# Another order, and another choice of engine, for the VectorE, ScalarE and GpSimd work of an attention, Fourier and MLP kernel

## The chip, the cores and the metric

The kernel runs on one core of one Trainium2 chip. A core has five engines with an instruction queue each: TensorE (PE in the profile, with its weight loads as PEld), VectorE (DVE), ScalarE (ACT), GpSimd (POOL) and SyncE (SP), which here issues nearly all DMA transfers. Each engine works through its own list strictly in order, and waits at semaphores for what other engines and transfers make. The metric is the device time of the whole program in microseconds (us).

## The reference

First comes attention with random features, for 8 batches and 8 heads of 576 positions by 64; then a Fourier mix of its output over positions and channels, a normalisation, and an MLP of 512 to 2048 to 512:

```
def phi(x):
    proj = np.einsum('bhsd,md->bhsm', x, omega)
    sq = np.sum(x * x, axis=-1, keepdims=True) / 2.0
    h = proj - sq
    h = h - np.max(h, axis=-1, keepdims=True)
    return np.exp(h) / np.sqrt(m)
...
num = np.einsum('bhsm,bhmd->bhsd', q_p, kv)
den = np.einsum('bhsm,bhm->bhs', q_p, z)[..., None] + 1e-06
...
X = np.fft.fft(x, axis=1)
X = np.fft.fft(X, axis=2)
u = x + np.real(X)
...
ch = np.maximum(un @ w_ch1, 0.0) @ w_ch2
return (u + ch).astype(np.float32)
```

The two weight matrices come as 64-bit floats, and the kernel turns them into 32-bit ones itself.

## The kernel before

The program has two parts. The first (to about 433 us in the profile) does the attention for 32 pairs of heads, the Fourier mix of 8 batches, the conversion of the weights, the MLP of the first four tiles of 128 rows (called plain), and the preparation of the weights for the second part. The second part does the MLP of the other rows with a recursive product scheme that saves multiplications (lines from 1640 on). The change touches the first part alone.

Nothing in the first part is a plain loop. Each piece of work is a generator that yields steps; a step names the engines that it may run on with a planned cost for each, the events that it waits for, the buffers and PSUM banks that it takes and gives back, and the event that it makes. The planner (class `Listing`, method `run`) holds one step of every open stream in a list, and writes steps down one by one; when it writes a step, the code behind the `yield` issues the step's instructions. In the first part it does not choose: the string PICKS says which stream comes next and which of the step's engines takes it, one character for each step. A character's index in DIGITS is divided by 36: the remainder is the place of the stream in the list, the quotient the engine in the step's own order. So PICKS fixes the order of every engine's queue. Planned costs then matter no more; the chip's waits come from semaphores that follow from what each step reads and writes. BANKS fixes, in the order of the takes, which PSUM bank is used.

The steps that the change and the prediction speak of:

- Transposes of a pair's k and q rows and of its features on TensorE (L608), copied out of PSUM in blocks by `evicted` (L622 and L624), on ScalarE or VectorE; `kqT` and `qeT` are the results.
- Feature products (L702), then in `softmax` the row maximum on VectorE (L645) and the exponentials on ScalarE (L662, four for a group).
- k-features times v (L736), kept by `keep` (L750 VectorE, L752 ScalarE); numerators and denominators (L783, L791); the division (L800 to L812).
- `narrow`: the conversion of one slab of 512 weight columns, of 32. Its first step scales the high words (L533 GpSimd, or L535 ScalarE), three steps on VectorE treat the bits (L538, L540 and L543, L545), and the last adds (L551, GpSimd or VectorE). It reads the tile `raw`, one of four slab buffers, and the last step gives the buffer back. The load of a later slab (L565, SyncE) waits for a buffer.
- `folds`: sums and differences over mirrored positions and channels ahead of the Fourier products (L839, L845, L855, L868), VectorE or GpSimd; the products (L897 to L945); copies of the spectra on ScalarE (L918).
- `residual` and `summed`: the spectrum is mirrored and added to x (L989 on ScalarE, L994 and L997 on VectorE, L1006 and L1007 on VectorE or GpSimd), then written to DRAM (L976, L1021, L1032, SyncE).
- Normalisation of a tile (L1163 to L1169), its transposed rows `unT` (L1177), the first MLP layer (L1237), its copies in `hidden` (L1221 VectorE, L1223 ScalarE), the second layer (L1260).
- `op` in `w2_parts`: differences of the second weight matrix for the second part (L1485, VectorE or GpSimd).

SyncE's list interleaves the loads of k and q (L472, L475, two buffers), of v (L480, three buffers), of the slabs, and the traffic of the mix. A load that must wait for a buffer holds back all that stands behind it. Some preparation for the second part is started after given numbers of listed steps (the string BETWEEN); all of those numbers lie past the region that the change touches.

Of the kernel before, what the change touches and what calls it, by code (L numbers as in the profile page):

```python
# [41 lines left out]
class Clock(NamedTuple):  # L42
# [23 lines left out]


PICKS = (
    "40e0fff03eafdaege3OcdceefdcOdeccfgda37ghj0gjj7hlP79aj7ik97i8S7efhjffeHldffiehdjfdOihgihidaKedbhhciff"
    "ecgOfeejdfdPdeeedgifdffdefd8aiii88jhd8jP8b99i8e8jcddghjgheiifcOcdciieicgPgdefJcdghbkededfgcRbggb79ij"  # L70
    "8hi7hjafN9Haj9gfffeg8eif8hcej1jccc7ehidbhffLigebfbe6766gggfcbjahj9Ofghhjj8dQkkgT6jghff8de6dUjfhbgegh"
    "cefhafjUf8jgciSjOckkhjakkaeikggjlioklnhSgodoXON7l7l6nnj9icadc97cibf98ejH88a7edhMlhkmjjaQVijihkkfplSm"
    "okliljjilVaghVhnmljkmpjkhhnmkimlgglmbjpjjQ9d9alafhhdjlaMdjback0j766k7lh4g896ck6gkki77gij5ijhgj6dimni"
    "3ndjgi6Kc4jldlKikbkaijLhf75dcjlmklk36ci45jciekajkkkk5kihokeaeoLaioNlencidonbSiljjcmjjkboijTUUhgcfkik"
    "hiflkmeFF99nol5m8jT7naabda89Rbj97ecdl8cjilOgifkQb4acahg57ebbgabgdjkdTkk6eceebb5f9dg4R6ce486ggg6egfhh"
    "fg4g9egf5cbdhgPRhhcgjhggejigibLmHnbedijj6NOb7biihi9bgihMkaffPa8cijdhbdghbaeibNefffacjicigifi99975ih5"
    "jgj8699ajfg6g7fgefd65bO6Kalkkgd5jgjikagfldliPJpeoaeeefgdejadgilgScljiii5e65k56kl57k7j67S9lilk9gliih6"
    "ffkgec4fg4dbgg7fedaiP5gfbheefilddddddeghg9kbfncgghcfkkafkagGngb65p5Hopoj4bhoanbelli68bjjl5b7dlhighhi"
    "lflhpkgiWomjknmmmkimnjbjhn9jkmFKkfFgedccff6Wf7idUVhi8Th3fogbqp8fgmkeSdjna7ckenoghmnmffnjeo79q6547oa4"
    "nlkpd7aceonnc8blSVicilbhmjim8fh7SnnIl5mUkfjgfhhfhihg8ghfbS4kjf83j4lllb79jei8mnkblfnmmiolpilOUi9Mh5l5"  # L80
    "pmnaem79jjVmkbblek5iji9a9kffTgjikhiShfgjafhgfigh4g50PPP0ba5Pdh9dghdK77hgfdcbg8OO988jMehefibjjkellfcc"
    "PcdhQMihfQcffbKCf82b3c98cbcdcd6a299efgddbJaGQQbefLa9ecf74gg986HRgf9idg8kQeheff7be6ff2e5cc8fbcgdKP8f8"
    "9hN9Lc999bddcHcNb7Oc9effegd7ibhQeQ8haf7ccghhlUikhHW5lWmm5dkMQGM71fS6d1gdb99747ifddhIfdhhdhfdbihgiljn"
    "gWgijgg93ekKl8kEhIIbT3jjKgkb9k9eTfhkhlje34m49974iG66h68faHe6e7a79982975aI94a39c8cM8b4aa7ab984fge8eLM"
    "98b86ce8PbFPc9cbe6cKPf3a9b94fIdIQeJKbd876eJPdc5fNb7ffbf9JSS8RiLa4a7gPbajfgg8gdfhg2i2787Hf6OcdIN5d3LH"
    "accd46ddeKK72dJc7bbaa4bb9a9bc7c0777dghhdf7Bfddebd76ff1fddIe9949438686bc6aca85348dHcG7a5be957b55d1544"
    "9Gc1F5a9a68446344584584E59189970955888574443113301110"
)
# [2307 lines left out]
```

## Time and profile before

| what | value |
|---|---|
| median of 3 runs | 1124.67 us (1122.62 to 1125.05) |
| the profiled execution | 1126.43 us |
| its span, first to last instruction | 1124.6 us |
| granted TensorE clock | 1.000 |
| first part, 0 to 433 us: TensorE busy | 422.68 us |
| the same: VectorE, ScalarE, GpSimd busy | 353.31, 306.46, 192.19 us |

The profile is one execution. Its page gives the busy time of each engine, groups of instructions by line and tile, and the chain of work that ended last; the trace behind it answers for stretches of time, for single lines and for waits. A row of the timeline reads: start in us, length in us, engine, line, operation, what it writes and reads, shapes, how many; in brackets the idle time before it and what ended that. Matmul ends are modelled, so a busy TensorE still holds short stalls.

### The profile page before, as it was taken

To read this page: it belongs to the slowest core of one execution; us is meant where nothing else is said; L and a number is where in the kernel's file an instruction comes from. 1 tells how busy PE (TensorE), PEld (TensorE's weight loads), DVE (VectorE), ACT (ScalarE), POOL (GpSimd) and SP (SyncE) were. 2 spreads that over 40 slices of the span, in tenths; PEclk is the share of its full clock that TensorE was granted. 3 is DMA by queue.
4 is the path that set the end of the run, shared out by engine and by line. 5 is a ranking of instruction groups with operands and counts; after the bars stand their busy time and mean duration, and the time that the engine had idled before them with its cause. 6 is when DMAs were issued, how large, how long until landed. Compare 5 with 4: busy or idle time off the path is not lost.

```text
span 1124.6 us, 31666 instructions
## 1 busy us (share of the span) xinstructions
PE 1109.1 (99%) x12467; PEld 1000.3 (89%) x12467; DVE 887.5 (79%) x1684; ACT 540.6 (48%) x1644; POOL 389.5 (35%) x402
## 2 busy tenths in 40 slices
PE   8999999999999999999999999999999999999998
PEld 7888888879869678899999889999889999889998
DVE  6999999987676766687697777888667898668895
ACT  7998898856635465624214553223563222341221
POOL 2443443644473347633513454000365000142000
PEclk9999999999999999999999999999999999999999
DMA  8866766565675659798898768757778757546553
GB/s 234 217 194 181 229 188 211 156 206 166 215 231 183 191 164 317 239 301 277 240 297 287 215 203 255 201 155 234 208 209 250 219 156 218 165 155 216 150 160 105
DMA packets 196549, 236.13 MB, mean 210 GB/s; under 512 B 53808, under 2 KB 120624, under 8 KB 196400
## 3 DMA queue, kind: packets, MB, share of 16 engines
q1 hardware_dynamic: 195904, 233.83, 68.7%
q8 instruction: 99, 1.62, 0.6%
q14 instruction: 50, 0.41, 0.1%
q10 hardware_dynamic: 496, 0.26, 0.1%
HBM read 182.13 MB, written 56.10 MB: 212 GB/s over the span
## 4 chain that ended last, share of the span: by engine, by line
PE 88%; DVE 3%; DMA 3%; ACT 3%; POOL 1%; issue 1%; SPq 1%; DVEq 0%; POOLq 0%; ACTq 0%
PE banks L2179 30%; PE banks L1728 26%; PE banks L1237 5%; PE banks L702 5%; PE banks L608 4%; PE banks L1879 3%; PE banks L1260 3%; PE banks L736 2%; PE banks L783 2%; PE banks L945 2%; DMA raw<-in_moe_w_ch_dram 1%; PE banks L895 1%; ACT e L662 1%; DVE nmx L645 1%; PE banks L905 1%
## 5 line engine op out<-in xcount | busy, mean ns | idle before, releaser
L2179 PE MATMUL banks<-wl,sums 128*128 128x128 f32 x1792 | 219.8, 275 | 0.5 <-issue 0.5
L2179 PEld LDWEIGHTS banks<-wl,sums 128*128 128x128 f32 x1792 | 210.6, 192 | 1.5 <-issue 0.9
L662 ACT ACTIVATE e<-banks,nmx 128x128 f32<-128x128 f32 x576 | 165.2, 429 | 25.0 <-DVE nmx L645 24.3
L645 DVE TENSOR_REDUCE nmx<-banks 128x8 f32<-128x1024 f32 (+1 forms) x96 | 89.2, 950 | 17.6 <-PE banks L702 13.4
L2179 PE MATMUL banks<-wl,hid 128*128 128x128 f32 x768 | 99.2, 275 | 0.3 <-DVE part L2155 0.3
L2179 PEld LDWEIGHTS banks<-wl,hid 128*128 128x128 f32 x768 | 92.9, 192 | 0.9 <-DVE part L2155 0.5
L2150 ACT ACTIVATE s<-banks 128x128 f32<-128x128 f32 x112 | 30.9, 277 | 113.6 <-PE banks L2179 103.5
L1728 PE MATMUL banks<-unw,wxw 128*128 128x256 f32 x352 | 85.5, 379 | 0.0
L702 PE MATMUL banks<-om,kqT 64*64 64x128 f32 (+1 forms) x2088 | 78.7, 275 | 2.2 <-ACT kv L752 1.4
L702 PEld LDWEIGHTS banks<-om,kqT 64*64 64x64 f32 (+1 forms) x2088 | 64.1, 138 | 13.2 <-issue 3.4
L2179 PE MATMUL banks<-wl,hx 128*128 128x128 f32 x576 | 74.2, 275 | 0.4 <-DVE part L2155 0.4
L1728 PEld LDWEIGHTS banks<-unw,wxw 128*128 128x128 f32 x352 | 66.6, 190 | 8.9
L1728 PE MATMUL banks<-rx,wxw 128*128 128x256 f32 x288 | 70.8, 379 | 0.0
L1753 ACT ACTIVATE s<-banks 128x512 f32<-128x512 f32 x65 | 38.5, 596 | 65.9 <-PE banks L1728 60.8
L2179 PEld LDWEIGHTS banks<-wl,hx 128*128 128x128 f32 x576 | 69.4, 192 | 0.8 <-DVE part L2155 0.6
L1728 PE MATMUL banks<-ttw,wxw 128*128 128x256 f32 x288 | 69.8, 379 | 0.0
L1237 PE MATMUL banks<-unT,w 128*128 128x128 f32 x512 | 65.4, 279 | 1.7 <-DVE qeT L622 1.7
L551 POOL TENSOR_TENSOR w<-w,raw 128x512 f32<-128x512 f32 x28 | 37.6, 1351 | 78.2 <-DVE raw L545 78.2
L1237 PEld LDWEIGHTS banks<-unT,w 128*128 128x128 f32 x512 | 60.2, 192 | 4.4 <-issue 2.3
L2228 POOL TENSOR_TENSOR more<-more,part 128x512 f32<-128x512 f32 x2 | 2.6, 1315 | 176.7 <-ACT part L2221 176.7
L1728 PEld LDWEIGHTS banks<-ttw,wxw 128*128 128x128 f32 x288 | 54.5, 190 | 7.3
L1728 PEld LDWEIGHTS banks<-rx,wxw 128*128 128x128 f32 x288 | 54.5, 190 | 7.3
(287 smaller groups left out, 2439.2 us busy)
## 6 DMA issues: line engine op xcount, KB each, us to landing
wl<-w2l SPq DMA_DIRECT2D x245, 256.0 KB, 3.9
wxw<-w1x SPq DMA_DIRECT2D x120, 256.0 KB, 3.2
raw<-in_moe_w_ch_dram SPq DMA_DIRECT2D x32, 512.0 KB, 5.6
kq<-in_k_dram SPq DMA_DIRECT2D x32, 288.0 KB, 4.5
kq<-in_q_dram SPq DMA_DIRECT2D x32, 288.0 KB, 4.8
vd<-in_v_dram SPq DMA_DIRECT2D x32, 288.0 KB, 5.3
ur<-us SPq DMA_DIRECT2D x30, 256.0 KB, 5.1
w2l<-sums SPq DMA_DIRECT2D x14, 512.0 KB, 4.4
```

Source lines behind the costliest of these rows:

```text
L551: eng.tensor_tensor(out=dst, in0=dst, in1=lof, op=ALU.add)
L608: nc.tensor.transpose(ps[:, (j - j0) * 128 : (j - j0 + 1) * 128], src(j), ident[:])
L645: nc.vector.tensor_reduce(nmx[:, :, 0:num], pps[:, :, 0 : MF * num].rearrange("p b (c m) -> p b c m", m=MF), axis=AX.X, op=ALU.max, negate ...
L662: nc.scalar.activation(out=e[:, c + (i if num == 1 else 0), :], in_=pps[:, i, MF * c : MF * c + MF], func=AF.Exp, bias=nmx[:, i, c : c + 1],)
L702: nc.tensor.matmul(pps[cols, c, MF * m : MF * m + MF], lhsT=kqT[rows, j, cols], rhs=om2[rows, :],)
L1237: nc.tensor.matmul(hp[:, 0:TP], lhsT=w1[:, dc, 128 * fc : 128 * fc + 128], rhs=unTs[key][:, dc, :], start=(dc == 0), stop=(dc == NDC - 1),)
L1260: nc.tensor.matmul(yp[:, 0:DM], lhsT=hs[fc][:, 128 * i : 128 * i + 128], rhs=w2[:, fc, :], start=(fc == 0), stop=(fc == NFC - 1),)
L1728: nc.tensor.matmul(ps[:, span * f : span * f + span].rearrange("f (b q) -> f b q", q=Q), lhsT=left[:, P * f : P * f + P], rhs=right, start ...
L1753: nc.scalar.activation(out=s[:], in_=ps, func=AF.Copy)
L1879: nc.tensor.matmul(cell.rearrange("f t (b q) -> f t b q", q=Q), lhsT=w[:, d, col : col + 128], rhs=right[:, :, d].rearrange("f (t b) q -> ...
L2150: nc.scalar.activation(out=s[:], in_=ps[:, 0:128], func=AF.Copy)
L2179: nc.tensor.matmul(ps[:, 0:128], lhsT=left[:, f], rhs=wls[head(j), i, n][:, f], start=start and f == 0, stop=(f == 3), skip_group_check=True,)
```

## The change

The string PICKS gets other characters; BANKS, BETWEEN and everything else stay. The steps themselves are the same. VectorE, ScalarE and GpSimd get many of them in another order, and 115 of them go to another of the three engines: mostly first steps of `narrow` from ScalarE to GpSimd, `evicted` copies from ScalarE to VectorE and some back, `hidden` copies both ways, and folds, sums and differences from VectorE to GpSimd and some back. The order of TensorE's and SyncE's steps is as before. The core of the diff (the first two of the lines that differ, of 17):

```
 PICKS = (
-    "40e0fff03eafdaege3OcdceefdcOdeccfgda37ghj0gjj7hlP79aj7ik97i8S7efhjffeHldffiehdjfdOihgihidaKedbhhciff"
-    "ecgOfeejdfdPdeeedgifdffdefd8aiii88jhd8jP8b99i8e8jcddghjgheiifcOcdciieicgPgdefJcdghbkededfgcRbggb79ij"
...
+    "40e0fff03eafdaegN3cMcceedecOdeccfgda37ghj0gjj7hlQf7H89iik7887ePehjPefjefehdfeekgePgefPhdKfKdfcbhdiee"
+    "ddbfNeddicdhgfgfeccdegddcce8jjj88ki8dlQ9acaj9f8kdeeihhjfgRghiddedjfkjRhfgghfgijegl8cJejgdfcRbgb79jk8"
...
```

More of the change, by code (lines that the diff above doesn't have):

```diff
@@ L68 @@
 PICKS = (
-    "40e0fff03eafdaege3OcdceefdcOdeccfgda37ghj0gjj7hlP79aj7ik97i8S7efhjffeHldffiehdjfdOihgihidaKedbhhciff"
-    "ecgOfeejdfdPdeeedgifdffdefd8aiii88jhd8jP8b99i8e8jcddghjgheiifcOcdciieicgPgdefJcdghbkededfgcRbggb79ij"
-    "8hi7hjafN9Haj9gfffeg8eif8hcej1jccc7ehidbhffLigebfbe6766gggfcbjahj9Ofghhjj8dQkkgT6jghff8de6dUjfhbgegh"
-    "cefhafjUf8jgciSjOckkhjakkaeikggjlioklnhSgodoXON7l7l6nnj9icadc97cibf98ejH88a7edhMlhkmjjaQVijihkkfplSm"
-    "okliljjilVaghVhnmljkmpjkhhnmkimlgglmbjpjjQ9d9alafhhdjlaMdjback0j766k7lh4g896ck6gkki77gij5ijhgj6dimni"
@@ L74 @@
[L74 to L83, printed above, removed]
@@ L84 @@
-    "gWgijgg93ekKl8kEhIIbT3jjKgkb9k9eTfhkhlje34m49974iG66h68faHe6e7a79982975aI94a39c8cM8b4aa7ab984fge8eLM"
-    "98b86ce8PbFPc9cbe6cKPf3a9b94fIdIQeJKbd876eJPdc5fNb7ffbf9JSS8RiLa4a7gPbajfgg8gdfhg2i2787Hf6OcdIN5d3LH"
+    "40e0fff03eafdaegN3cMcceedecOdeccfgda37ghj0gjj7hlQf7H89iik7887ePehjPefjefehdfeekgePgefPhdKfKdfcbhdiee"
+    "ddbfNeddicdhgfgfeccdegddcce8jjj88ki8dlQ9acaj9f8kdeeihhjfgRghiddedjfkjRhfgghfgijegl8cJejgdfcRbgb79jk8"
+    "ij7ika79O8Lajf9gefe8fjf8icfk1kkeddhgijfdigNlb6Ndgeb877gggfGHaj9k8OJeheigjj7cPghii6jiffeefaeefgbheiej"
@@ new lines @@
+    "OefaekglidjTkQellikcllafjlhhkmjplmoIMM9M9KbManiLdek7g7i6kkedfa76jb6f6fjaac6fiNmilnkkc7QVHhihgkkepSUi"
+    "lojkjkUiiVgigUhnmllkpLVpijggnmihmlfflmkpaQii9c69k9fhgdiUhddcbcj0i655j7kg47e89bjbih6ij7hij5ijhfj6cimn"
+    "3cONiencoacdd4ffbahiLfjfj75g7eilmmkk56hjlHN3Qelaklmll5ljiiocacploaQOlfmfpnnUkmjcjenjmdpikWUjkhgnOF5d"
+    "ggjfgdkmbbno95m8b7n9acb8ba9QjL897cecej7bihcddgjPa4dch9h56eaag9hejkebSjk5b78j8hk4dU7798ce486ggg6egffg"
+    "gg49fegfdcfgPSiidhNFHbe6geccakjhj9c9mSgfMQdeigggfiQH8adihebffPe8iLhNhadegbadcbNeLddaagabcRjiS8jcdb75"
@@ new lines @@
+    "hg5ifi69agh67ghgfe65HFMcm5kkQdJhJikeek9adckbkhbeTRl5eedfej9dgmKMVQRebmkgjTd65l56lm5a6k8Ialilka8lihh7"
+    "ffkgec4fge4ibghfRIeHc9g4feagddehkafceccjh8lafobdhghbbejjfkagoLNaKdd65o5oogi4gnbdj67Nc56ejekeka6elhid"
+    "ohhifmhplgjpnljnoNhjljjSklaigmjkl8jhfefff7FVe7hcWUgihTh3hbqi6nVggf8Udk7cmegem8omhmgknmPido78q6546o95"
+    "nlkpad9ceVYamllb8aklanjjil8gfn6fnmQm6kOfjeT7hTdiig8hi4k834ckelimmd7bLRb9Okgfmml7kndnmkVlpklXh5f5qeob"
+    "gnielFdT5Ik8fgiajiii99khgljjkiahhficShfjgfggfgih4g40PPPEO0a94Pdh8dgh56hg8edcg89eNO98eiehefibeiikilPK"
@@ L86 @@
+    "TcNebbbgfiLRggefa782c3ca9cbcdcd62aaefgaccccd9daFN9bcecf74gg986HRgf98hcffOiegg7bMe6ff2e5cc8fbHJKgeb7f"
+    "788QO9b8888added7cdb9effegc7iajhePhbai7ccghmTUPgjgHV5k5UV6UIUfab717c1gea88646ifddag7Occgfdahgfhkimfd"
+    "doQPMWWldeec3blf89NTk3dfheKTPVkh9jbacgPVhiffjg434k48975g69fIae6ee8Lba2K76aa4a39c8c8c5bbK7ab985fg8JgK"
+    "bMb886c8fbabDecbe6MLPf3aN9b94fegJIP5aI765J7ebbagOd7ffcf8ISS9RiLa4a8gPbajfgg8gdfhg2i2787Hf6OcdIN4d3LH"
     "accd46ddeKK72dJc7bbaa4bb9a9bc7c0777dghhdf7Bfddebd76ff1fddIe9949438686bc6aca85348dHcG7a5be957b55d1544"
```

## The prediction

> **What bounds the kernel now.** I read the page's engine line first, then the busy time by stretches of 27 us, then TensorE's waits, then the timelines of the places named there. TensorE is all but full, in the first part too; what a new order of the other engines can win is the time that TensorE stands still for them.
>
> ```profile
> PE 1109.1 (99%) x12467; PEld 1000.3 (89%) x12467; DVE 887.5 (79%) x1684; ACT 540.6 (48%) x1644; POOL 389.5 (35%) x402
> ```
>
> By stretches (TensorE, weight loads, VectorE, ScalarE, GpSimd, clock, DMA share, GB/s), two of the first part: VectorE and ScalarE are nearly as full as TensorE, GpSimd is not.
>
> ```profile
> 81.00:108.00 27.00, 25.86 (x565) 21.37 (x559) 25.74 (x58) 25.36 (x92) 9.25 (x11) 1.00 0.66 198
> 162.00:189.00 27.00, 26.57 (x546) 23.13 (x544) 24.93 (x64) 23.27 (x83) 11.62 (x11) 1.00 0.71 211
> ```
>
> TensorE's own waits between 24 and 100 us: ScalarE ends most of them.
>
> ```profile
> PE banks L702 <- ACT kv L752: 1.4, 3, 0.7
> PE banks L608 <- ACT e L662: 0.9, 3, 0.4
> PE banks L783 <- ACT qeT L624: 0.5, 1, 0.5
> ```
>
> The one long wait after 216 us, and the VectorE work ahead of it. Those operations take about twice their usual time (L839's usual 1.22 us is 2.28 here):
>
> ```profile
> 331.26 1.96 PE L1237 MATMUL banks<-unT,w 128*128 128x128 f32 x15 [1.69 <-DVE qeT L622]
> ```
> ```profile
> 324.04 1.49 DVE L1169 TENSOR_SCALAR u<-u,mv,rstd 128x512 f32<-128x512 f32 x1
> 325.45 2.28 DVE L839 TENSOR_TENSOR half<-x 128x1024 f32<-128x1024 f32 x1
> ```
>
> The start. The first weight slab lands at 14.79; the queues that wait for it stand still with all behind it.
>
> ```profile
> 14.79 1.53 POOL L533 TENSOR_SCALAR w<-raw 128x512 f32<-128x512 f32 x1 [13.39 <-DMA raw<-in_moe_w_ch_dram]
> ```
> ```profile
> 14.81 0.91 DVE L538 TENSOR_SCALAR sign<-raw 128x512 uint32<-128x512 uint32 x1 [2.34 <-DMA raw<-in_moe_w_ch_dram]
> ```
>
> One VectorE operation of 512 columns by its extremes (minimum, median, maximum ns); it is long where GpSimd runs beside it:
>
> ```profile
> L538 DVE TENSOR_SCALAR sign<-raw x32: 364/427/1526, 14.8 to 243.2; 128x512 uint32<-128x512 uint32 x32
> ```
>
> SyncE, in order: slab 17, then the mirrored rows, then the return copy, then the q half of pair 15.
>
> ```profile
> 118.90 0.33 SPq L565 DMA_DIRECT2D raw<-in_moe_w_ch_dram  x1
> 120.37 1.25 SPq L976 DMA_DIRECT2D uh<-x  x2
> ...
> 126.09 0.57 SPq L1032 DMA_DIRECT2D us<-uh  x1
> 128.01 0.59 SPq L480 DMA_DIRECT2D vd<-in_v_dram  x1
> 128.64 1.47 SPq L475 DMA_DIRECT2D kq<-in_q_dram  x1
> ```
>
> **The change, part by part.** Followed character by character through the planner's streams, both strings list the same steps; TensorE's 498 and SyncE's 195 stand in the same order, and no moved step issues a DMA. All differences run between about 5 and 354 us. So the matrix work costs what it did, and the change is worth the TensorE stalls that it takes away or adds.
>
> What is carried over, to 216 us: the first step of a net 13 slabs goes from ScalarE (0.75 us, L535) to GpSimd (1.54, L533); 12 net PSUM copies from ScalarE to VectorE (0.3 to 0.8 us each); folds and residual sums from VectorE (0.75 to 1.2) to GpSimd (1.35 to 2.4). By mean durations of those rows ScalarE sheds 17.8 us of 218, VectorE 3.5 of 208, GpSimd takes 35.8 more on 87. After 216 us what is moved nearly cancels but for 297 to 324 us, where GpSimd's list grows from 16.0 to 22.5.
>
> (a) Start: +2.0. The first step of slab 0 goes from GpSimd to ScalarE, listed before the two groups of four exponentials of pair 0 that ran at 11.04 and 12.04. ScalarE now waits for the landing at 14.79, then 0.75, then the groups at 1.15 each: done at 17.8 instead of 13.3. The transposes that ran at 13.33 read them, so TensorE loses 4.4 us there. It wins back the 0.7 before L608 at 16.37 and the gap of 1.1 before 19.33, which lie inside the new wait. By ScalarE's next steps (three exponential groups, two copies) pair 0's numerators start near 22.4 instead of 20.43. Bounds: +1.0 (copies overlap better) to +3.2 (the 1.1 gap comes again).
>
> (b) ScalarE's relief, 24 to 100 us: -3.2. Six slab steps leave ScalarE here (0.75 each, and at 76.63 a 0.8 wait for a landing with the exponentials and copies queued behind it). TensorE's waits that ScalarE ends are 2.8 us in its matmul row, 6.4 in the row of weight loads. I take half of the larger, near the smaller, since VectorE, no emptier, ends the wait next. Bounds: -6.4 to 0.
>
> (c) GpSimd's queue and the slabs, 109 to 141 us: +4.5. On GpSimd the first step of slab 14 now stands ahead of slab 10's last, and that of slab 15 ahead of the last steps of 11 and 13. Each last step frees the slab for a later load, and SyncE's loads keep their order. If slab 14 lands as now (113.65): 1.54, then slab 10 (1.30) is free at 116.5, so load 15 issues 4.7 late; landing 5.6 later at 122.1; 1.54, a residual sum 1.4, slabs 11 and 13 at 1.30 each: load 17 issues near 127.7 instead of 118.90. Of the 8.8 us, 1.1 was SyncE's wait for a sum; the rows below it slip 7.7: the q half of pair 15 issues at 136.3, lands 4.9 later at 141.2, and TensorE's transposes that read it ran at 135.8. That is +5.4; if load 14 goes out when its slab allows, it is +3.2. I take 4.5, nearer the reading from the rows as they stand. Lower bound 0: GpSimd ahead of its list or TensorE late anyway.
>
> (d) Collisions of VectorE with GpSimd: +2.5. VectorE operations on SBUF alone (L538 to L545, folds, sums) are long beside GpSimd; those on PSUM (L645, 1.21 us) are not. Before, 17 of the 99 us of such work to 216 us ran beside GpSimd, and was 10 us longer than the shortest of its shapes. GpSimd's busy share there goes from about 0.4 to 0.57; at the same avoidance that is some 21 us beside it, 2.5 us dearer, less the 3.5 shed: -1 on VectorE. Where it can't be avoided: from 81 to 189 us (108 us) GpSimd and such VectorE work list 72.4 + 47.6 = 120.0 us, 98.7 before. If none may overlap, the queues end 11.8 late. VectorE is over 92% busy there, so what it loses TensorE soon loses. Bounds -2.0 to +11.8; 2.5 is near the low end, since the two do overlap in rows of before (14.81).
>
> (e) The wait at 331.26: -1.7. It waits for the copy of pair 28's first transposed block, behind VectorE's doubled operations. That copy goes to ScalarE, listed right behind the transposed rows (L1177, 327.0) that L1237 needs anyway. What is late next are those rows: a spectrum's copy of some 0.9 us is now listed ahead of them, so they come near 328, before TensorE is free at 329.6. Bounds -1.7 to 0.
>
> The rest (20 hidden-layer copies swapped between ScalarE and VectorE at 0.28 to 0.30 us, GpSimd's crowding at 297 to 324 us) I cost at nothing: after 216 us ScalarE and VectorE have idle time, and the second part starts 70 us later. If that cover goes, it costs one GpSimd step, 1.3 us.
>
> Sum: 2.0 - 3.2 + 4.5 + 2.5 - 1.7 = +4.1. The profiled execution took 1126.43 (span 1124.6 and 1.8 around it): 1130.5. It lay 1.76 above the median of 1124.67, so 1128.8 as a median.
>
> **The rivals.** *The relief pays in full* (faster): with ScalarE 8% and VectorE 2% lighter, (b) reaches -6.4 and (d) -2.0: -3.6, 1121.1. For it: ScalarE is what TensorE waits for to 100 us. Against: VectorE stands behind it, as full. It decides once (b) and (d) together pass -7.1.
>
> *GpSimd and VectorE take turns* (slower): (d) is +11.8: +13.4, 1138.1. For it: L538 at up to 1526 ns, and the doubled rows at 324 us. Against: at 14.81 L538 ended inside GpSimd's 1.53. [...]
>
> *The late transfer is hidden* (no change): (c) is 0: -0.4, 1124.3. For it: one buffer of lead, and 4.9 us to landing is within a queue's scatter. Against: q of pair 15 landed only some 2 us before it was read.
>
> **How the numbers follow.** Forecast 0.42 (own range 1125.5 to 1132), relief 0.26, turns 0.18, hidden 0.14. This kernel's measurement can tell about 0.2%, 2.25 us. Slower: 0.36 of the forecast's 0.42 and turns, 0.54. Same: 0.12 of hidden and the forecast's 0.06, 0.18. Faster: relief and the 0.02 left of hidden, 0.28. The range, 1119 to 1138, goes past relief and up to turns; it leaves out some 0.2.
>
> **What would show it.** (a) ScalarE idle from 10.7 to 14.8 and TensorE still near 13.4 to 17.8. (b) Fewer waits on ScalarE between 24 and 100 us. (c) Load 17 near 127, TensorE waiting for q at 136 to 141. (d) L538 and folds more often over 0.8 us. (e) No wait at L1237 near 331. The forecast is wrong if TensorE reaches 216 us's work no later than now, and its sign is (b) against (c) and (d).

## The result and the profile after

The changed kernel takes 1157.98 us (median of 6 runs, 1154.65 to 1161.09) against 1123.72 for the kernel before (6 runs beside it): a ratio of 1.0304, 95% interval 1.0282 to 1.0326. It is slower by 34 us; the forecast was 4 us slower, and the range ended at 1138.

The first line of the page of the changed kernel, busy time by engine, and two stretches of its first part (TensorE, weight loads, VectorE, ScalarE, GpSimd, clock, DMA share, GB/s):

```profile
PE 1121.3 (97%) x12467; PEld 1007.6 (87%) x12467; DVE 911.1 (79%) x1690; ACT 528.7 (46%) x1617; POOL 445.0 (39%) x432
```
```profile
81.00:108.00 27.00, 22.02 (x463) 17.56 (x461) 22.87 (x41) 19.39 (x70) 13.55 (x11) 0.87 0.67 201
162.00:189.00 27.00, 25.71 (x540) 22.06 (x538) 26.52 (x55) 20.41 (x77) 17.41 (x15) 1.00 0.52 150
```

ScalarE is lighter and GpSimd heavier, as forecast. TensorE is busy for 22.0 us of the first stretch instead of 25.9, and its granted clock there is 0.87: a quarter of the stretch ran at half clock. The kernel before had no half clock before its end. In this profile the clock was 0.5 at 97.8 to 104.6, 149.0 to 152.4, 193.3 to 196.7 and 350.3 to 353.8 us, 17.1 us in all. Half of that, 8.5 us, is my estimate of its cost; in the run delays a wait of 3.05 us and 3.4 us of half clock behind it cost 4.8.

TensorE's waits of the changed kernel between 24 and 105 us. ScalarE ended most of them before; now VectorE and a load do:

```profile
PE banks L702 <- DVE kv L750: 2.2, 1, 2.2
PE banks L608 <- DMA kq<-in_q_dram: 2.1, 1, 2.1
PE banks L608 <- ACT e L662: 1.1, 3, 0.4
```

The order of TensorE's steps is the same in both kernels, so each step has one partner, and the difference of their starts (the lag) tells where the time went. By the step's start in the kernel before, in us (called TensorE's work below); the columns behind the first belong to experiments below, all against the same profile of before:

| work at | changed | changed, second profile | prefix_45 | vector_longer | both_back |
|---|---|---|---|---|---|
| 20 | -1.4 | +3.0 | +2.6 | -2.2 | +0.8 |
| 81 | -0.5 | +4.1 | +1.1 | 0.0 | +5.6 |
| 110 | +6.0 | +10.4 | +1.1 | +2.1 | +9.9 |
| 134 | +8.1 | +10.8 | +0.3 | +2.7 | +9.1 |
| 150 | +14.4 | +20.3 | +0.3 | +2.7 | +9.5 |
| 216 | +21.0 | +27.0 | -0.5 | +6.1 | +17.5 |
| 300 | +25.8 | +32.0 | -0.8 | +10.5 | +22.2 |
| 400 | +28.4 | +34.3 | -0.8 | +16.4 | +23.8 |

In the first profile all of it arises in the first part, in steps of 1.5 to 6 us from 80 us on; after 335 us nothing is added. (The second profile loses 3 us more at the start.) The largest step is the one at 135.8 us. SyncE and TensorE of the changed kernel there (slab 17, mirrored rows, return copy, v, q half of pair 15, and the transposes that read it):

```profile
133.46 0.33 SPq L565 DMA_DIRECT2D raw<-in_moe_w_ch_dram  x1
133.84 1.25 SPq L976 DMA_DIRECT2D uh<-x  x2
...
142.02 0.57 SPq L1032 DMA_DIRECT2D us<-uh  x1
142.63 0.63 SPq L480 DMA_DIRECT2D vd<-in_v_dram  x1
143.31 0.72 SPq L475 DMA_DIRECT2D kq<-in_q_dram  x1
```
```profile
148.56 0.99 PE L608 MATMUL banks<-ident,kq 128*128 128x128 f32 x5 [4.53 <-DMA kq<-in_q_dram]
```

The wait of 1.69 us at L1237 (the row at 331.26 before) is gone; TensorE's row of the changed kernel there:

```profile
359.69 2.51 PE L1237 MATMUL banks<-unT,w 128*128 128x128 f32 x21
```

The slab step L538 by its extremes; the median rose from 427 to 522 ns, the longest from 1526 to 2548:

```profile
L538 DVE TENSOR_SCALAR sign<-raw x32: 409/522/2548, 12.8 to 266.1; 128x512 uint32<-128x512 uint32 x32
```

How VectorE and GpSimd meet in the changed kernel, at 91 to 95 us: GpSimd's rows, VectorE's rows, and TensorE waiting for the copy behind them.

```profile
90.87 2.36 POOL L839 TENSOR_TENSOR half<-x 128x1024 f32<-128x1024 f32 x1 [0.23 <-DVE mid L875]
93.18 1.75 POOL L551 TENSOR_TENSOR w<-w,raw 128x512 f32<-128x512 f32 x1
```
```profile
91.77 2.01 DVE L540 SCALAR_TENSOR_TENSOR w<-w,sign 128x512 uint32<-128x512 uint32 x1
93.81 1.40 DVE L543 TENSOR_SCALAR sign<-w 128x512 uint32<-128x512 uint32 x1
95.25 0.69 DVE L545 SCALAR_TENSOR_TENSOR raw<-raw,sign 128x512 f32<-128x512 uint32 x1
```
```profile
98.34 1.99 PE L702 MATMUL banks<-om,kqT 64*64 64x128 f32 x32 [2.17 <-DVE kv L750]
```

L540 usually takes 0.68 us. It starts 0.9 us into GpSimd's fold and ends 0.55 after that fold's end; L543 (usually 0.43) ends 0.3 after GpSimd's next step. To put a number on this over the first part I took every VectorE record on SBUF alone (slab steps, folds, sums, L1169, L1485) less the shortest of its line and shape in the profile of before. This *lengthening* adds up to 20.6 us before and 49.1 after; of such work 38 us lay beside GpSimd before, 101 after. To the work of 216 us alone: 10.6 and 28.0, with 17 and 59 beside GpSimd.

Shared out by the GpSimd step that ran beside it, 9.0 of the 28.5 us more fall to L551, of which GpSimd has 28 as before; 7.5 fall to L1006 and L1007 (31 of each for 27), 6.1 to four more folds (L839), 4.3 to L1485, and only 1.6 to L533, of which GpSimd has 14 more. So the loss lies more in where the two engines' steps meet than in how many of them GpSimd was given.

### The profile page after: what moved, and what is told of

It reads as the page before. It is cut to its first block, busy times and chain, and to the rows that moved or that the text cites. A ratio compares the mean times of both kernels' runs of the same rounds, so it can differ in the third digit from the quotient of the medians.

```text
span 1152.9 us, 31639 instructions
## 1 busy us (share of the span) xinstructions
PE 1121.3 (97%) x12467; PEld 1007.6 (87%) x12467; DVE 911.1 (79%) x1690; ACT 528.7 (46%) x1617; POOL 445.0 (39%) x432
## 4 chain that ended last, share of the span: by engine, by line
PE 81%; DVE 9%; DMA 3%; ACT 2%; issue 2%; POOL 2%; SPq 1%; DVEq 0%; POOLq 0%; ACTq 0%
PE banks L2179 30%; PE banks L1728 26%; PE banks L702 4%; PE banks L1237 4%; PE banks L608 4%; PE banks L1879 3%; PE banks L1260 3%; PE banks L783 2%; PE banks L736 2%; DVE nmx L645 2%; ACT e L662 1%; PE banks L945 1%; PE banks L895 1%; DMA kq<-in_q_dram 1%; DVE w L540 1%
## 5 line engine op out<-in xcount | busy, mean ns | idle before, releaser
L662 ACT ACTIVATE e<-banks,nmx 128x128 f32<-128x128 f32 x576 | 162.8, 411 | 42.3 <-DVE nmx L645 42.0
L645 DVE TENSOR_REDUCE nmx<-banks 128x8 f32<-128x1024 f32 (+1 forms) x96 | 89.2, 949 | 13.4 <-PE banks L702 12.3
L1237 PE MATMUL banks<-unT,w 128*128 128x128 f32 x512 | 66.6, 282 | 0.0
L1237 PEld LDWEIGHTS banks<-unT,w 128*128 128x128 f32 x512 | 61.7, 196 | 2.6 <-issue 1.9
L1260 PE MATMUL banks<-w,ht 128*128 128x512 f32 x128 | 60.8, 614 | 0.2 <-DVE w L551 0.2
L1728 PEld LDWEIGHTS banks<-ttw,wxw 128*128 128x128 f32 x288 | 54.5, 190 | 7.3
L1728 PEld LDWEIGHTS banks<-rx,wxw 128*128 128x128 f32 x288 | 54.5, 190 | 7.3
```

The source lines that it names most:

```text
L645: nc.vector.tensor_reduce(nmx[:, :, 0:num], pps[:, :, 0 : MF * num].rearrange("p b (c m) -> p b c m", m=MF), axis=AX.X, op=ALU.max, negate ...
L662: nc.scalar.activation(out=e[:, c + (i if num == 1 else 0), :], in_=pps[:, i, MF * c : MF * c + MF], func=AF.Exp, bias=nmx[:, i, c : c + 1],)
L1237: nc.tensor.matmul(hp[:, 0:TP], lhsT=w1[:, dc, 128 * fc : 128 * fc + 128], rhs=unTs[key][:, dc, :], start=(dc == 0), stop=(dc == NDC - 1),)
L1260: nc.tensor.matmul(yp[:, 0:DM], lhsT=hs[fc][:, 128 * i : 128 * i + 128], rhs=w2[:, fc, :], start=(fc == 0), stop=(fc == NFC - 1),)
L1728: nc.tensor.matmul(ps[:, span * f : span * f + span].rearrange("f (b q) -> f b q", q=Q), lhsT=left[:, P * f : P * f + P], rhs=right, start ...
```

## The experiments

Followed through the planner, the two lists differ in the engine of 116 steps (not 115, as told above), 19 of them copies of the hidden layer (the prediction has 20). The first two runs ask whether the loss goes with the engines (G) or with the places (O). Then two theories were set against each other. X: the changed lists put GpSimd's operations beside VectorE's, VectorE stands still, and TensorE waits for what comes behind. M: the list of before is dovetailed, and steps out of place make TensorE's feeders late whatever their engine. Later half clock (K) was added. Kernels that mix both lists keep TensorE's and SyncE's order; their edit is other characters in PICKS, of which the first changed line is shown. All results in one table (lengthening and half clock from the one profile of each; the ratio's interval in brackets):

| kernel | us | ratio to before | lengthening, us | at half clock, us |
|---|---|---|---|---|
| before | 1123.7 | 1 | 20.6 | 0 |
| changed | 1157.98 | 1.0304 (1.0282 to 1.0326) | 49.1 | 17.1 |
| changed_again | 1157.05 | 1.0293 (1.0273 to 1.0314) | 47.5 | 27.3 |
| engines_only | 1159.52 | 1.0325 (1.0310 to 1.0341) | 42.3 | 23.9 |
| places_only | 1164.38 | 1.0362 (1.0344 to 1.0379) | 35.7 | 20.5 |
| slabs_undone | 1154.11 | 1.0276 (1.0261 to 1.0292) | 44.7 | 20.5 |
| prefix_45 | 1127.06 | 1.0033 (1.0020 to 1.0046) | 20.8 | 6.8 |
| load_wide | 1135.35 | 1.0101 (1.0087 to 1.0116) | 32.8 | 6.8 |
| load_tiny | 1137.80 | 1.0121 (1.0106 to 1.0136) | 29.3 | 6.8 |
| vector_longer | 1143.25 | 1.0161 (1.0130 to 1.0192) | 23.3, and 29.0 put in | 3.4 |
| undo_vector_gpsimd | 1151.93 | 1.0229 (1.0180 to 1.0279) | 39.9 | 13.7 |
| undo_scalar_vector | 1166.52 | 1.0367 (1.0339 to 1.0395) | 49.7 | 27.3 |
| undo_scalar_gpsimd | 1149.02 | 1.0212 (1.0183 to 1.0242) | 44.9 | 13.7 |
| undo_gpsimd_all | 1149.07 | 1.0220 (1.0191 to 1.0250) | 36.3 | 13.7 |
| fold_on_vector | 1153.87 | 1.0276 (1.0256 to 1.0295) | 45.7 | 13.7 |
| both_back | 1149.90 | 1.0234 (1.0212 to 1.0256) | 44.7 | 13.7 |
| kept_busy | 1156.39 | 1.0284 (1.0265 to 1.0302) | 49.0 | 10.2 |
| qe28_on_act | 1123.65 | 0.9998 (0.9988 to 1.0008) | 18.2 | 0 |
| clear_321 | 1124.26 | 0.9998 (0.9989 to 1.0007) | 20.1 | 0 |
| delays | 1139.62, one run | | 18.6 | 10.2 |

### Engines and places apart

engines_only, against before:

```
-    "40e0fff03eafdaege3OcdceefdcOdeccfgda37ghj0gjj7hlP79aj7ik97i8S7efhjffeHldffiehdjfdOihgihidaKedbhhciff"
+    "40e0fff03eafdaege3eMdMeefdcOdeccfgda37ghj0gjj7hlf79ajHik97S8S7efhjffeHldffiehdjfdOShgihidKKedbhhciff"
...
```

> Every step stands where the kernel before has it, and the 116 steps go to the engine that the changed kernel gives them. The change cost 34 us in all. Theory G, the moves cost: GpSimd's greater load on SBUF and in its queue makes VectorE late, wherever the steps are listed; then this kernel takes most of the loss, 20 to 34 us (1144 to 1158). Theory O, the places cost: single steps stand too far back in a queue, or behind a wait; then this kernel takes under 10 us (1116 to 1134). TensorE at half clock: by either theory only where TensorE waited for over 2 us just before.

places_only, against before:

```
-    "40e0fff03eafdaege3OcdceefdcOdeccfgda37ghj0gjj7hlP79aj7ik97i8S7efhjffeHldffiehdjfdOihgihidaKedbhhciff"
+    "40e0fff03eafdaegd3ccMceedecOdeccfgda37ghj0gjj7hlQP7789iik7887efehjPefjefehdfeekgePgeffhdafKdfcbhdiee"
...
```

> Every step stands where the changed kernel has it, and goes to the engine that the kernel before gives it. Theory G: under 10 us of the 34 (1116 to 1134). Theory O: 20 to 34 us (1144 to 1158). If each of the two alone costs much more than its share (together well over 34), neither order nor engines is bad by itself, and it is the fit of the one to the other that matters.

Measured: 36 and 41 us slower. Each half alone costs as much as both together; neither theory's split came true, and the third outcome written down did. It matters how engines and places fit each other. Even without one step more for GpSimd, the new places raise the lengthening from 20.6 to 35.7.

### The start

prefix_45, against before:

```
-    "40e0fff03eafdaege3OcdceefdcOdeccfgda37ghj0gjj7hlP79aj7ik97i8S7efhjffeHldffiehdjfdOihgihidaKedbhhciff"
+    "40e0fff03eafdaegN3cMcceedecOdeccfgda37ghj0gjj7hlQf7H89iik7887ePehjPefjefehdfeekgePgefPhdKfKdfcbhdiee"
...
```

> The changed kernel's list up to TensorE's work of 45 us in the kernel before, and from there the list of the kernel before; 11 steps on another engine. In the traces the changed kernel was 2.0 us ahead there. Theory L, lags add up and nothing later gives them back: 2 us faster than the kernel before, 1121 to 1123, and TensorE 2 us ahead from 45 to 430. Rival, the slack is given back (TensorE next waits for a load, or for VectorE, that is no earlier): 1123 to 1125, the lead gone before 216 us.

> The changed kernel once more, unaltered, for a second profile of it. In the first one slab 0 had landed at 12.1 us, and TensorE was 1.4 us ahead of the kernel before at 20 us; in the other kernels that begin with the same list it was 0.6 to 2.6 us behind. Theory S, the first was an early landing and term (a) holds for the usual one: here ScalarE waits until 14 to 15 us and TensorE is 1.5 to 3.5 us behind at 20 us. Rival: it is ahead again, and the list costs nothing at the start. Half clock: behind the same three waits as before (149, 193, 349 us), if the windows fall alike. Time 1155 to 1161.

prefix_45 is 4 us slower than before, where 2 us faster or no change was expected. (Its one profile is of the fastest of its runs, 1125.63, and has caught up by 216 us, so it does not show where the 4 us went.) The lead of the first profile was an early landing of slab 0. In the second profile of the changed kernel ScalarE waits longer for that slab, with the exponentials behind it, and TensorE for them; the first step of slab 0, then TensorE:

```profile
13.55 0.68 ACT L535 ACTIVATE w<-raw 128x512 f32<-128x512 f32 x1 [2.49 <-DMA raw<-in_moe_w_ch_dram]
```
```profile
15.30 1.12 PE L608 MATMUL banks<-ident,kq 128*128 128x128 f32 x4 [2.66 <-ACT e L662]
```

In the first profile that step ran at 12.10, after a wait of 0.98. At 20 us, ten profiles with ScalarE's slab 0 ahead of the exponentials lag the profile of before by 1.3 us in the mean (-1.5 to +3.0); nine in which GpSimd treats that slab where the kernel before lists it, that one among them, are ahead of it by 1.2 (0 to 2.2). So the list costs some 2.4 us at the start, and an early landing in one run is not its gain.

Nearly all of these 2.4 us are half clock. In eight of the ten profiles TensorE waited 1.5 to 3.4 us there, and half clock of 3.4 or 6.8 us followed (the four transposes at 15.30 take 1.12 us, in the first profile 0.66); half of that, the estimate of its cost, is 2.0 us in the mean of the ten. In the other two, the changed kernel's first profile and kept_busy, the wait was 1.2 and 1.3 us, no half clock followed, and TensorE is ahead of before by 1.4 and 1.5, as with the old list.

### The slabs in GpSimd's queue

slabs_undone, against the changed kernel:

```
-    "OefaekglidjTkQellikcllafjlhhkmjplmoIMM9M9KbManiLdek7g7i6kkedfa76jb6f6fjaac6fiNmilnkkc7QVHhihgkkepSUi"
+    "OefaekglidjTkQellikcllafjlhhkmjplmoIMM9M9KbManiLdek7g7i6kkedfa76cib6e6ej99b6fiNmilnkkb7QVijihkkfpSUi"
...
```

> The changed kernel, with the steps of slabs 10 to 17 alone (narrow) at the places and on the engines of the kernel before; six of them change engine. Theory C, GpSimd's order of the slab steps is what holds back SyncE's loads and the q half of pair 15: TensorE's wait of 4.7 us at 148.6 and the 3.4 us at half clock behind it go, 6.4 us less than the changed kernel (near 1151.5); the issue of load 17 comes at some 6 us less behind the kernel before. Rival: the loads are late because TensorE and the slabs' VectorE steps are late; then under 2 us is won and the wait stays near 4 us.

TensorE's row at the transposes of pair 15's q in slabs_undone:

```profile
148.39 1.15 PE L608 MATMUL banks<-ident,kq 128*128 128x128 f32 x9
```

The wait of 4.53 us and the half clock behind it are gone: the lag stays between 13.0 and 13.9 from the work of 105 to 140 us, where the changed kernel's grew by 8. Load 17 goes out at 132.30; it is 13.4 us later than before, as late as TensorE itself, instead of 14.6 at a lag of 7. Theory C holds for the place. In time it brought 3.9 us of the 6.4 expected; this profile began 4.4 us behind the other at 20 us and had half clock at other places. The brackets of the two kernels in the table overlap a little, so it is the rows that show the place and not the time alone.

### More work for GpSimd, nothing moved

load_wide and load_tiny, against before:

```
         eng.tensor_tensor(out=dst, in0=dst, in1=lof, op=ALU.add)
+        if step.eng == POOL:
+            nc.gpsimd.tensor_scalar(dst, dst, 1.0, None, op0=ALU.mult)
```
```
         eng.tensor_tensor(out=dst, in0=dst, in1=lof, op=ALU.add)
+        if step.eng == POOL:
+            for _ in range(7):
+                nc.gpsimd.tensor_tensor(dwell[:], dwell[:], dwell[:], op=ALU.mult)
```

> The kernel before, and behind each of the 28 last steps of narrow on GpSimd one more GpSimd operation of 128 x 512 in place (w times 1.0), some 1.45 us each, 41 us in all: as much as the change gave GpSimd (35.8). Nothing is listed elsewhere. Theory X, collisions: VectorE's operations on SBUF alone stand still while a GpSimd operation of this width runs; about half of the 41 us falls on such work, so VectorE's records grow by 8 us or more and the kernel by 8 to 25 us (1131 to 1148). Theory Q, lateness in GpSimd's own queue: the same loss here and in load_tiny. If neither holds, under 3 us.

> As load_wide, but in place of the operation of 128 x 512 seven of 128 x 1 (0.19 us each by the row L1604): GpSimd is occupied as long and its next step comes as late, but no single operation lasts over 0.2 us. Theory X: VectorE's records stay about as long as before, and the kernel within 4 us of it (1121 to 1127). Theory Q: the loss of load_wide within 3 us.

11.0 and 13.5 us slower. GpSimd got 44.8 us by the first edit and 54.5 by the second, as the small operations took 0.28 us each; lines in these two kernels are shifted by 2 and by 5:

```profile
L553 POOL TENSOR_SCALAR w<-w 128x512 f32<-128x512 f32 x28 | 44.8, 1599 | 2.4
```
```profile
L556 POOL TENSOR_TENSOR dwell<-dwell 128x1 f32<-128x1 f32 x196 | 54.5, 278 | 13.2
```

By the words written down, theory Q (lateness in GpSimd's queue) fits better than X: the two losses lie within 3 us, and VectorE's lengthening rose in both, by 12.2 and 8.7 us. But the pair does not part the theories. In load_tiny the 45 VectorE records of this kind that had nothing but small operations beside them were 1.1 us longer in all; the rest arose beside the kernel's own GpSimd steps, which came later and met VectorE more often. So small operations did VectorE little harm, as X says, and lateness in GpSimd's queue made new collisions, as Q and X say together. What the pair does show: as much GpSimd time as the change added, put in blindly, costs a third of what the change cost.

### VectorE made slower, nothing moved

vector_longer, against before; LONGER holds 38 numbers of listed steps with 1 to 9 operations each, at the steps that GpSimd had lengthened in the changed kernel:

```
+            for _ in range(self.longer.pop(placed, 0)):
+                self.filler()
             go_on(item)
...
+    listing.filler = lambda: nc.vector.tensor_reduce(dwell[:], ident[:], axis=AX.X, op=ALU.max)
```

> The kernel before, list and engines untouched, with VectorE made as slow as it was in the changed kernel: at the 38 VectorE steps that GpSimd lengthened there by over 0.16 us more than before, 103 small VectorE operations (a maximum over 128 x 128, some 0.27 us each) stand ahead of the step, 28 us in all; the profile of the changed kernel had 49.1 us of such lengthening against 20.6. Theory X, the lengthening by itself makes the loss: 20 to 34 us slower than before (1144 to 1158), half clock behind the long waits. Theory M, the lists are dovetailed and it is the misfit of order that costs: under 14 us (below 1138), since VectorE's idle time takes the rest.

What was put in, by the groups of its trace:

```profile
L1638 DVE TENSOR_REDUCE dwell<-ident 128x1 f32<-128x128 f32 x103 | 29.0, 282 | 2.3
```

18.0 us slower: between the two theories. VectorE late by 29 us costs TensorE 16 to 18, so some 0.6 us for each, 1.7 of half clock included. By this price the changed kernel's 28.5 us of lengthening make about 16 of its 34. On this estimate theory X is right on half of the loss, and wrong as the whole of it.

### Groups of steps put back

Each against the changed kernel, first undo_vector_gpsimd, then undo_scalar_vector, then undo_scalar_gpsimd and undo_gpsimd_all (which have the same first line):

```
-    "ij7ika79O8Lajf9gefe8fjf8icfk1kkeddhgijfdigNlb6Ndgeb877gggfGHaj9k8OJeheigjj7cPghii6jiffeefaeefgbheiej"
+    "ij7ika79O8Lajf9gefe8fjf8icfk1kkeddhgijfdigNlb6Ndgeb877gggfG7aj9k8OJeheigjj7cPghii6jiffeefaeefgbheiej"
...
-    "40e0fff03eafdaegN3cMcceedecOdeccfgda37ghj0gjj7hlQf7H89iik7887ePehjPefjefehdfeekgePgefPhdKfKdfcbhdiee"
+    "40e0fff03eafdaeg3dOcdceedecOdeccfgda37ghj0gjj7hlQf7979iik78i87eehjPefjefehdfeekgePghefhdKfKdfcbhdiee"
...
+    "40e0fff03eafdaegN3cMcceedecOdeccfgda37ghj0gjj7hlPP7H89hik7887ePehjPefjefehdfeekgePgefPhdafKdfcbhdiee"
...
```

> The changed kernel, with the 32 steps that change between VectorE and GpSimd (folds, sums, last steps of narrow, differences) at the places and on the engines of the kernel before. Theory X: these put GpSimd's work beside VectorE's and take the larger part: 12 us or more less than the changed kernel (below 1146). Theory M: what is put back no longer fits what is left; within 6 us of the changed kernel (1152 to 1164).

> The changed kernel, with the 66 steps that change between ScalarE and VectorE (copies out of PSUM, the hidden layer's copies) at the places and on the engines of the kernel before. Theory X: GpSimd is not touched, so within 6 us of the changed kernel (1152 to 1164). Rival V, it is the copies given to VectorE that make it late: 10 us or more less (below 1148).

> The changed kernel, with the 18 first steps of narrow that change between ScalarE and GpSimd at the places and on the engines of the kernel before: GpSimd has 14 of them less, 21 us by the mean of row L533 in the kernel before. Theory X: 8 us or more less than the changed kernel (below 1150), VectorE's lengthening well under 49 us. Theory M: within 6 us of it (1152 to 1164).

> The changed kernel, with all 50 steps that enter or leave GpSimd at the places and on the engines of the kernel before; the 66 changes between ScalarE and VectorE and the other places stay. Alone, the 32 brought 6 us and the 18 brought 9 us. Theory X: GpSimd has its old load at its old times, VectorE's lengthening falls from 49 to under 32 us, and the two gains add up or more: 15 us or more less than the changed kernel (below 1144). Theory M: what is left is as ill-fitted; 1148 or more.

6 us less (with single runs from 1144.5 to 1157.1, so unclear), 8.5 us more, 9 us less, and 9 us less with both GpSimd groups. The last one goes against X: GpSimd was back at its old load, yet the lengthening only fell to 36.3 and 25 us of the loss stayed. That the ScalarE and VectorE changes make it worse when taken out alone suggests that they fit the other moves. undo_scalar_gpsimd met its time, but its lengthening was still 44.9, so its 9 us are not shown to come from collisions (L533 had only 1.6 us of the lengthening above). No group carries the loss.

### One step put back, and two places together

fold_on_vector, against the changed kernel (one line, one step); both_back adds it to slabs_undone:

```
-    "lojkjkUiiVgigUhnmllkpLVpijggnmihmlfflmkpaQii9c69k9fhgdiUhddcbcj0i655j7kg47e89bjbih6ij7hij5ijhfj6cimn"
+    "lojkjkUiiVgigUhnmllkmoLnijggnmihmlfflmkpaQii9c69k9fhgdiUhddcbcj0i655j7kg47e89bjbih6ij7hij5ijhfj6cimn"
```

> The changed kernel with one of its steps put back: the 128 x 1024 fold of batch 1, second half (L839, GpSimd, 2.36 us at 90.87), on VectorE and at the place of the kernel before. In the changed kernel the VectorE step of slab 10 (L540, usually 0.68) stood still behind it until 93.2, the next (L543) behind the last step of slab 9 until 94.9, and the copy that TensorE waited for (2.17 us at 98.3) came behind those, with half clock to 104.6. Theory X: VectorE is 1.5 us or more earlier there although it takes the fold (1.14) itself; the step at 95 to 105 us in TensorE's lag, 5.3 us with the half clock, falls to under 2; in all 2 to 5 us less than the changed kernel (1153 to 1156). Theory M: VectorE is as late with the fold as behind it; within 1.5 us of the changed kernel (1156.5 to 1159.5).

> The changed kernel with two of its parts put back together: the steps of slabs 10 to 17 and the one fold of batch 1. Alone they brought 3.9 and 4.1 us. Theory A, located losses add up, each at its place: 7 to 9 us less than the changed kernel (1149 to 1151). Theory M, each repair shifts what comes after against the rest of the list and part is lost again: 1152 or more.

VectorE and TensorE of fold_on_vector at the place shown above:

```profile
93.69 0.68 DVE L540 SCALAR_TENSOR_TENSOR w<-w,sign 128x512 uint32<-128x512 uint32 x1
94.40 0.43 DVE L543 TENSOR_SCALAR sign<-w 128x512 uint32<-128x512 uint32 x1
94.74 1.22 DVE L839 TENSOR_TENSOR half<-x 128x1024 f32<-128x1024 f32 x1
```
```profile
98.96 1.10 PE L702 MATMUL banks<-om,kqT 64*64 64x128 f32 x32 [0.89 <-DVE kv L750]
```

VectorE takes the fold itself and still is 1.3 us earlier against TensorE's work (L545 starts 0.6 us later, at a lag 1.9 larger), where 1.5 was expected: three operations in 2.3 us, where two took 3.4. TensorE's wait falls from 2.17 to 0.89, half clock stays away there, and the lag grows by 1.9 us from the work of 89 to 111 us instead of 5.7. Here X is shown at its place. By the medians it is 4.1 us less than the changed kernel, from one step of 116; the brackets of the two kernels overlap, so the time alone would not show it. both_back took 8.1 us off, the sum of 3.9 and 4.1, and its bracket lies apart from the changed kernel's: located losses added up.

### Two tries at the wait of 331 us in the kernel before

qe28_on_act and clear_321, against before:

```
-    "gWgijgg93ekKl8kEhIIbT3jjKgkb9k9eTfhkhlje34m49974iG66h68faHe6e7a79982975aI94a39c8cM8b4aa7ab984fge8eLM"
+    "gWgijgg93ekKl8kEhIIbT3jjKgkb9k9efhlhhlje34m49974iG66h68faHe6e7a79982975aI94a39c8cM8b4aa7ab984fge8eLM"
```
```
-    "gWgijgg93ekKl8kEhIIbT3jjKgkb9k9eTfhkhlje34m49974iG66h68faHe6e7a79982975aI94a39c8cM8b4aa7ab984fge8eLM"
+    "gWgijgg93ekKl8klllEhIIbT3jjKgkb9k9eTfhkhlje34m49974i77h79fbIe7e88aa92a86aa4a39c8cM8b5aa7ab985fge8eLM"
...
```

> The kernel before, with one step of the change alone: the copy of the first transposed block of pair 28 on ScalarE, right behind the transposed rows of the normalisation. Term (e): TensorE's wait of 1.7 to 1.9 us at 331 us goes and nothing gives it back, 1.7 us less (1121.5; ratio 0.9985). Rival: what is won at 331 is lost again at the next copy or load before 430 us, within 0.5 us of the kernel before.

> The kernel before with three differences of the second weight matrix (L1485: two from GpSimd, one from VectorE itself) on VectorE at 318.7, where it stood idle for 2.2 us; GpSimd's row of five from 321 to 329 us becomes three. In the kernel before each VectorE operation from 321.3 to 328.9 ended with a GpSimd one. Theory X: L839 and L841 at 325 to 329 go back from 2.28 and 1.23 to 1.2 and 0.2, the copy that TensorE waits for at 331 and the row maximum behind it come 2 us earlier, and the wait of 1.86 us goes: 1.7 us less than the kernel before (ratio 0.9985). Rival: the wait moves to another step, as it did when the copy alone was moved; ratio 0.9995 or more.

Both 0.9998: nothing. TensorE's row in qe28_on_act, and VectorE's fold with TensorE's row in clear_321:

```profile
328.50 0.71 PE L1237 MATMUL banks<-unT,w 128*128 128x128 f32 x4 [1.71 <-ACT e L662]
```
```profile
324.53 2.28 DVE L839 TENSOR_TENSOR half<-x 128x1024 f32<-128x1024 f32 x1
326.74 0.16 DVE L841 COPY half<-x 128x2 f32<-128x2 f32 x1
```
```profile
329.32 2.96 PE L1237 MATMUL banks<-unT,w 128*128 128x128 f32 x24 [1.34 <-DVE qeT L622]
```

In the first, TensorE ran eight more matmuls of the layer and then waited as long, now for the exponentials behind the row maximum (L645), which itself stands behind the doubled VectorE operations. In the second GpSimd's next difference moved forward into the gap, so the fold still took 2.28 us; only L841 was freed.

### Half clock

delays, against before (the copy is called as often as the table says):

```
+AGAIN = {("qeT", 20, 0): 5, ("qeT", 24, 1): 4, ("qeT", 26, 1): 6, ("qeT", 30, 1): 9}
...
+            for _ in range(AGAIN.get(step.makes, 1)):
+                copy(dst[:, i], of)
```

> The kernel before, with the copies of four transposed blocks of features repeated in place, so that TensorE has to wait: pair 20 block 0 five times, pair 24 block 1 four times, pair 26 block 1 six times, pair 30 block 1 nine times (at 225, 260, 302 and 352 us of the kernel before). Theory K, a wait of TensorE over some 2.1 us is followed by 3.4 us at half clock, which costs another 1.7: half clock after the waits of over 2.2 us (that of nine copies, near 5 us, for certain) and none after those under 1.9. Rival: half clock comes with something else of the changed kernel (many small groups, DMA), and none is seen here. Time: the sum of the waits and 1.7 for each drop, near 1131 to 1142.

kept_busy, against the changed kernel:

```
+            for _ in range(self.warm.pop(placed, 0)):
+                self.warmer()
             go_on(item)
...
+    listing.warm = {664: 24, 1514: 12}
+    listing.warmer = lambda: nc.tensor.transpose(banks[:, listing.got.ids[0], 0:128], ident[:], ident[:])
```

> The changed kernel, with 24 transposes of a constant (0.11 us each) on TensorE ahead of the transposes of pair 15's q that it waits 4.5 us for at 148.6, and 12 ahead of the feature products it waits 2.5 us for at 349, written to the bank that the step overwrites. Theory K, TensorE's clock is halved for the next 3.41 us by a window of 3.41 us in which it was busy for under half: with the waits filled there is no half clock behind these two, and none is lost by the filling; 3 us less than the changed kernel (near 1155). Rival, the clock answers to the waiting itself or to what the other engines do: half clock at both places as before, and 0 to 1 us more than the changed kernel.

TensorE's waits in delays from 220 to 375 us (line numbers shifted):

```profile
PE banks L707 <- DVE qeT L625: 4.4, 1, 4.4
PE banks L1265 <- ACT qeT L627: 3.0, 1, 3.0
PE banks L741 <- DVE qeT L625: 2.1, 1, 2.1
```

In this profile half clock followed the waits of 3.05 us (3.4 us long) and 4.4 us (6.8 long), and none the waits of 2.1 and less. The lag grew by 4.8 over the wait of 3.05 and the half clock behind it: about the wait and half of 3.4.

In the profile of the changed kernel the eight changes of the clock from 97.75 to 353.75 us lie whole multiples of 3.4133 us apart, within 1 ns (2, 13, 1, 12, 1, 45 and 1 times), so windows of that grid can be laid over each profile. Two such windows in the changed kernel and two in kept_busy, around 350 us (columns as above: the ends, the length, then TensorE's busy time):

```profile
346.93:350.34 3.41, 1.38 (x11) 0.74 (x12) 3.38 (x9) 0.00 (x0) 1.41 (x3) 1.00 0.59 173
350.34:353.75 3.41, 3.41 (x6) 1.35 (x5) 3.41 (x7) 0.62 (x2) 3.41 (x2) 0.50 1.08 336
```
```profile
345.50:348.91 3.41, 3.22 (x23) 2.18 (x24) 3.41 (x10) 0.57 (x2) 2.11 (x1) 1.00 1.09 273
348.91:352.32 3.41, 3.41 (x15) 2.02 (x13) 3.40 (x3) 0.05 (x1) 3.41 (x4) 1.00 0.91 338
```

With the wait filled TensorE kept its clock (1.00 from 345.50 to 352.32). At pair 15's q it didn't: the load came later still, 2.8 us of transposes left 3.2 us of the wait, and half clock followed. In time kept_busy gained 1.6 us, within the spread of the runs; theory K rests on the windows. Over the first part of all 20 profiles, windows at full clock:

| TensorE busy in the window | windows | followed by half clock |
|---|---|---|
| under 45% | 40 | 40 |
| 45 to 60% | 49 | 13 |
| over 60% | 2376 | 1 |

## Why the prediction was wrong

The direction held, and so did the mechanisms of (c) and (d); the size did not, and (a) and (e) met theirs by luck. By the steps of the working:

- **(d), collisions: the step that failed most.** The term took GpSimd's busy share up from 0.4 to 0.57 "at the same avoidance": 21 us of such VectorE work beside GpSimd, 2.5 us dearer. Measured to the same work: 59 us, and 17.4 dearer (28.0 against 10.6). The avoidance was a property of the old list and did not survive; places_only lost much of it with no load added. (The planner's own `start` holds back a step marked `port` until the other of the two engines is done with its own; a list planned so would carry the avoidance. That is argued from the code, not shown.) After 216 us, where nothing was costed, another 11 us of lengthening came. At 0.6 us each, the measured price, the term is some 16 us. The upper bound of 11.8 fell with it, and so did the rival of turns (1138), which had the mechanism right in the main (beside L533 168 of 368 VectorE records ended before GpSimd's, see the last section).
- **Half clock: not in the working at all.** Waits were costed at their own length. 8.5 us in the first profile and 13.7 in the second come on top. The profile of before did not show it: its clock was 1.00 up to 1124.1 us, and its longest wait in the first part was 1.69 us.
- **(c), the slabs: right.** Forecast 4.5, or 5.4 by the rows as they stood; the lag grew by 4.7 and 5.3 in the two profiles, through the chain that was named, and slabs_undone took it away.
- **(a), the start: right in size by luck.** Forecast 2.0, measured 2.4 in the mean of profiles; the first profile of the changed kernel shows none of it. TensorE did wait for ScalarE's exponentials, as named, but for 1.2 to 3.4 us and not 4.4, and it won nearly all of that back, where the working let 2.0 stand. What stayed is almost all half clock, which the working did not have. The working took the landing at 14.79 as fixed; in 20 profiles GpSimd or ScalarE took slab 0 up between 11.8 and 14.8.
- **(b), ScalarE's relief: failed.** ScalarE's waits did go down, but nothing was won: by the page ScalarE itself now sat idle 42 us before the exponentials for VectorE's row maxima, 24 before. That VectorE "ends the wait next" stood in the text as a discount of half; it was the whole.
- **(e), the wait at 331: right in amount by luck.** It went (the lag fell by 1.9). But the copy that moved to ScalarE did not do it: alone, in qe28_on_act, it only moved the wait. In the changed kernel lengthened operations still stand ahead of the row maximum (L841 and twice L845, 1.5 to 1.8 us each, up to 356.39). TensorE itself came 4.5 us later, by the wait of 2.5 us at 349 and the half clock behind it. In fold_on_vector, slabs_undone and both_back, which have the same steps there but no half clock at that place, a wait of 1.5 us for a copy of VectorE's (L622) follows at the work of 334.6 and takes nearly all of the gain back.
- **"The rest at nothing": failed.** At the work of 173.8, 261.8 and 320.4 us the lag grew by 2.7, 1.6 and 2.8, at the first and the last behind copies on VectorE. The first lies in the stretch that (d) covers; at the others the idle time after 216 us that was to cover them was not where the waits were.

For the first profile, lengthening at the price of vector_longer without its half clock (28.5 by 0.5: 14), half clock 8.5, the q half 4.7 and (e) at -1.9 add up to about 26 of the 28.4. That is an estimate, as the parts are not independent. Open is why each half of the change alone loses more than both: the waits of places_only come at other places (6.6 us at one copy of pair 28), and its lengthening accounts for the smaller part. A step-by-step cause was shown only for the fold of batch 1 and the slabs, 8 of the 34 us. No version was faster than the kernel before beyond the noise.

## What to carry to other kernels

Where two engines hinder each other, as VectorE and GpSimd did here (49.1 us of lengthening for 20.6), the price of a new order is not in their busy shares: lay the records of both side by side, and take the avoidance in a tuned list as something that a move destroys unless the new list is checked for it. Cost a wait of TensorE with what follows it: here each of the 40 windows of 3.41 us with TensorE busy for under 45% was followed by half clock of 3.4 us or more, by estimate 1.7 us lost for each 3.4, and 12 idle transposes in the wait at 349 us kept the clock at 1.00 there. Compare several profiles before reading a lead of 2 us at the start as the kernel's own.

## What the runs showed of the hardware

- In the first part of the 20 profiles half clock followed all 40 windows of 3.41 us in which TensorE was busy for under 45%, 13 of the 49 with 45 to 60% and 1 of the 2376 above; 38 times it lasted one window, 16 times two to four. In the changed kernel a wait of 2.17 us at 98 us lay in a window with TensorE busy for 1.49 of 3.41 us, and half clock followed; one of 2.06 us at 85.5 left TensorE busy for 2.01 of 3.41 us in the window from 84.10, and none followed. One of 2.52 us ending at 192.64 left it busy for 0.89 of 3.41 us in one window, and half clock followed; in kept_busy its idle time at that place was split over two windows (busy for 2.96 and 1.60 of 3.41 us), and the clock stayed at 1.00.
- VectorE and GpSimd went in turns in some rows, two of them of small operations. In the changed kernel a copy of 128 x 2, 0.16 us by the median of the 11 with no GpSimd step beside them, started at 351.49 and ended 0.04 us after GpSimd's fold of 350.06 to 353.23:

```profile
351.49 1.78 DVE L841 COPY half<-x 128x2 f32<-128x2 f32 x1
```

  The other way round, a GpSimd operation of 128 x 1 in load_tiny, 0.19 us by its median, took 1.22 us at 50.40 beside VectorE's fold of 1.22 us at 50.35. How often it came so differed with GpSimd's operation. Of the VectorE records of the kinds counted as lengthening that started while an L551 (an addition of two tensors) ran on GpSimd, in all 20 profiles, 1 of 237 ended before it; of those that started beside an L533 (one tensor times a constant) 168 of 368 did. It differed with VectorE's too: L801 (128 x 10, on SBUF alone) took 216 to 219 ns in all 64 records of before and the changed kernel, and in before 9 of the 10 that started beside an L551 ended before it.
- The first step on slab 0, the first weight load, started anywhere from 11.8 to 14.8 us in the 20 profiles. The two profiles of the changed kernel, at 12.10 and 13.55, lay 4.4 us apart at 20 us, half clock behind the longer wait included.
